# Taking eleven masks off the matrix engine, and moving two small jobs from VectorE to GpSimd

## The chip, the cores and the metric

The kernel runs on one core of one Trainium2 chip. The metric is the device time of one execution in microseconds (us), as a median of several runs. The engines are named as in the profile: PE is TensorE's matmul, PEld its weight load, DVE is VectorE, ACT is ScalarE, POOL is GpSimd, SP is SyncE, whose queue issues all transfers.

## What is computed

Attention with a window of 32 positions in eight batches of eight heads (half of the heads plain, half with a dilation of 4), followed by a gated two-layer network on the resulting tokens. Cut to what matters:

```python
# q, k, v: (8, 8, 576, 64) float32
scores = matmul(q, k.transpose(0, 1, 3, 2)) / sqrt(64)
mask_plain = (rel >= 0) & (rel < 32)                       # heads 0 to 3
mask_dil = (rel >= 0) & (rel < 128) & (rel % 4 == 0)       # heads 4 to 7
scores = where(mask, scores, -1e9)
scores = scores - max(scores, axis=-1)
attn = exp(scores); attn = attn / (sum(attn, axis=-1) + 1e-9)
x = (attn @ v), heads side by side                         # 4608 tokens x 512
h = x @ w_in                                               # 512 x 2048
g = h * clip(h + 3, 0, 6) / 6
out = g @ w_out                                            # 2048 x 512
```

The products of the network are made in float32 precision from pairs: a number is a high word in TensorE's shorter format and a low word, its remainder, and a product is three matmuls (high by high, high by low, low by high).

## The kernel before

**Tiles.** Attention is cut into 48 units that the program calls trios (a batch, plain or dilated, and a third of the sequence). Since the window is 32, a trio needs only small blocks of scores: 24 products of 32 rows by 64 columns, which lie side by side in one PSUM bank of 128 x 384. The network's tokens are cut into 12 chunks of 384. The first four chunks go through both layers in the plain way (`gemm1`, `gemm2`); the other eight are taken two by two, in four groups, with seven products in place of eight for each two-by-two step (`first_product`, `multiply_right`). For that the weights are needed in sums and differences as well: for each side (`w_in` is 0, `w_out` is 1) and each of eight pairs of weight blocks, `combine` adds high and low words of two blocks (`combo_words`, twice), makes four sums (`combo_sum`), splits them again and writes them to memory, from where PE's later stage loads them into a ring of eight places (`ring`).

**Stages.** A beginning with an order written out by hand handles the first 12 trios, the conversion of the weights and most of the first two chunks; it ends near 150 us. Behind it, until about 333 us, come the remaining plain products, and at eight places (`SPOTS`) a block of two trios (`attend`). Then come the four groups; in the first three, one more trio's block stands beside each first product of a pair of weight blocks, until all 36 later trios are done. A block of trios also holds the weights-by-values products of the trios two numbers earlier.

**A later trio, step by step.** PE makes the scores (`mm_scores`, L228). The mask, 0 or -1e30, gets on in one of two ways: for the trios numbered in `PE_MASKS` (counted from 0 behind the first twelve) PE first multiplies the mask table by an identity into the same bank (L338), and the scores are summed on top; for the others VectorE adds the mask and writes the result to SBUF (`add_mask`, L254), which frees the bank. Then `scaled_largest` takes six maxima per row (L280) and multiplies them by minus the scale (L281), ScalarE makes six exponentials with these as bias (L289), VectorE transposes blocks (L385, L386), ScalarE copies the crossing blocks (L393), and the result `a` is read by PE (L246). For a trio in `PE_MASKS` the bank stays taken until the last exponential. The values' product goes the same way: shares, transposes, crossing copies to `xf`, and GpSimd's copies into a token block `raw` or a subtraction of high words (L454, L456).

**What sets the order.** Behind the beginning, every operation of the later stages is put on a list with its engine, an assumed duration, what it must follow, and the places in pools that it takes and gives. PE's order is the order of the list. For DVE, ACT, POOL and SP a planner (`_in_time`) walks through time and takes for each engine the operation that can start first, and among those the most urgent. So a change of an engine or of an assumed duration reorders the queues of all engines but PE. Each engine works strictly in its order: an instruction that waits holds up all that is behind it.

**On GpSimd before.** In the later stages it makes the high words of the plain chunks' gates (L557) and the copies of tokens, and nothing else.

Of the kernel before, what the change touches and what calls it, by code (L numbers as in the profile page):

```python
# [37 lines left out]
EVER = 1.0e6  # L38
SLACK = 0.4
SPOTS = ((35, 1), (38, 1), (41, 1), (44, 1), (47, 1), (50, 1), (53, 1), (56, 1))  # L40
SPARE = ((0, 1, 1, 2, 1, 1, 2, 1), (1, 1, 2, 1, 0, 0, 1, 1))
LEAD_SUMS = 300.0
# [1 line left out]
LATER = 2  # L44
LANDING = 2.6
EARLY = 90.0
PE_MASKS = frozenset((2, 5, 8, 9, 11, 12, 13, 14, 15, 20, 29, 36, 37))
SHARED = frozenset((0, 1, 2, 3, 4, 7, 8, 9, 10, 11, 12, 13, 14, 15, 27, 28, 32))
WIPED = set()
POOL_LOWS = frozenset((10, 11))  # L50
# [36 lines left out]
def windowed_attention_ffn(ctx: ExitStack, tc: tile.TileContext, qk, vp, w, mask, out, out_t):  # L87
# [23 lines left out]
    nc = tc.nc  # L111
# [17 lines left out]
    SCALE = 1.0 / math.sqrt(D)  # L129
# [3 lines left out]
    wpool = ctx.enter_context(tc.tile_pool(name="wpool", bufs=SLOTS_W))  # L133
    work = ctx.enter_context(tc.tile_pool(name="work", bufs=WORK))
    loads = ctx.enter_context(tc.tile_pool(name="loads", bufs=NLOAD))
    small = ctx.enter_context(tc.tile_pool(name="small", bufs=2))
    ps_h = ctx.enter_context(tc.tile_pool(name="ps_h", bufs=2, space=bass.MemoryType.PSUM))
    ps_a = ctx.enter_context(tc.tile_pool(name="ps_a", bufs=6, space=bass.MemoryType.PSUM))

# [44 lines left out]
    def w_tile(name, shape, dtype=F32):  # L184
        return wpool.tile([P, *shape], dtype, name=name, tag="w")
# [22 lines left out]
    pss, pvs, tps = {}, {}, {}  # L208
# [11 lines left out]
    def by_tensor(t):  # L220
        return t < NFIRST or t - NFIRST in PE_MASKS

# [28 lines left out]
    def add_mask(t):  # L251
        _, kind, part = trios[t]
        es[t] = work_tile("e")
        return nc.vector.tensor_tensor(out=es[t], in0=pss[t][0][:, :CH], in1=mask_sb[:, 3 * kind + part], op=ALU.add)  # L254
# [16 lines left out]
            in1=mx.rearrange("p (s o) -> p s o", o=1).broadcast_to([P, SLOTS, 2 * QB]), op=ALU.subtract,  # L271
        )

    def scaled_largest(t):
        ps, masked = pss[t]
        if not masked:
            ps = es[t]
        mx = small.tile([P, SLOTS], F32, name="mx")
        pss[t] = ps, mx, masked
        nc.vector.tensor_reduce(out=mx, in_=ps[:, :CH].rearrange("p (s x) -> p s x", x=2 * QB), axis=AX.X, op=ALU.max)  # L280
        nc.vector.tensor_scalar_mul(mx, mx, -SCALE)  # L281

    def exponents(t, j):
        ps, mx, masked = pss[t]
        if not j and masked:
            es[t] = work_tile("e")
        for i in (2 * j, 2 * j + 1):
            cols = slice(2 * QB * i, 2 * QB * (i + 1))
            nc.scalar.activation(es[t][:, cols], ps[:, cols], AF.Exp, bias=mx[:, i : i + 1], scale=SCALE)  # L289
# [242 lines left out]
    phs, ts, ghs, gls, po, done = {}, {}, {}, {}, {}, set()  # L532
# [99 lines left out]
    def combo_words(side, k, i, eng):  # L632

        if (side, k) not in combos:
            combos[side, k] = w_tile("v", [4, HALF])
        x, v = (win, wout)[side][2 * k + i], combos[side, k]
        eng.tensor_tensor(
            out=v[:, 2 * i : 2 * i + 2].rearrange("p a n -> p (a n)"), in0=x[:, 0].bitcast(F32), in1=x[:, 1].bitcast(F32), op=ALU.add
        )
# [151 lines left out]
    def op(engine, us, do, after=(), lag=0.0, takes=(), gives=(), before=(), ahead=AHEAD):  # L791
        plan.append(Operation(engine, us, do, [x for x in after if x is not None], lag, [(*x, 0)[:3] for x in takes], list(gives), list(before), ahead))
        if engine == "PE":
            beats.append(len(plan) - 1)
        return len(plan) - 1

    def transfer(us, size, do, after=(), takes=(), gives=(), ahead=EVER):
        x = op("SP", us, do, after, takes=takes, ahead=ahead)
        return op("DMA", size * 1.3, lambda: None, [x], lag=LANDING, gives=gives, ahead=EVER)
# [18 lines left out]
    def attend(bs, pools):  # L818

        scores = [NFIRST + b for b in bs if NFIRST + b < T]  # L820
        values = [NFIRST + b - 2 for b in bs if b >= 2]
        couples = [(NFIRST + b, NFIRST + b - 2) for b in bs]
        order = [t for x in couples for t in x if t in scores + values]
        bank, room = dict(zip(order, pools)), {}

        def do():
            for x in couples:
                block(*(t if t in bank else None for t in x), [bank.get(t) for t in x])

        names = {x: "ps_h" if bank[x] is ps_h else "ps_a" for x in order}  # L830
        for x in names.values():
            room[x] = room.get(x, 0) + 1
        beat = op(
            "PE", 0.35 + 0.3 * sum(by_tensor(t) for t in scores) + 0.535 * len(order), do,
            [*(x for t in values for x in turned[t]), *(landed_k.get(t) for t in scores), *(landed_v.get(t) for t in values),
             *(freed.pop(0) for _ in range(room.get("ps_a", 0)) if freed), *released["ps_h"][-2:][: room.get("ps_h", 0)]],
            takes=list(room.items()), gives=[("work", len(values))],
        )
        for ts in scores:
            if by_tensor(ts):  # L840
                x = op("DVE", 0.68, lambda ts=ts: scaled_largest(ts), [beat], ahead=EVER)
            else:
                x = op("DVE", 0.55, lambda ts=ts: add_mask(ts), [beat], takes=ONE, gives=[(names[ts], 1)], ahead=EVER)
                released[names[ts]].append(x)
                x = op("DVE", 0.68, lambda ts=ts: scaled_largest(ts), [x], ahead=EVER)
            for i in range(3):
                holds = not i and by_tensor(ts)
                x = op(
                    "ACT", 0.54, lambda ts=ts, i=i: exponents(ts, i), [x], takes=ONE if holds else (),
                    gives=[(names[ts], 1)] if i == 2 and by_tensor(ts) else (), ahead=EVER,  # L850
                )
            if by_tensor(ts):
                released[names[ts]].append(x)
            turned[ts] = turn_over(ts, es, ats, "a", x)
            if ts + NLOAD < T:
                landed_k[ts + NLOAD] = transfer(0.4, 0.82, lambda ts=ts: load_qk(ts + NLOAD), [beat])
        for tv in values:
            if tv - NFIRST in SHARED:
                x = op("DVE", 0.35, lambda tv=tv: share(tv), [beat], ahead=EVER)
                for i in range(3):  # L860
                    x = op(
                        "ACT", 0.5, lambda tv=tv, i=i: shares(tv, i), [x], takes=() if i else ONE,
                        gives=[(names[tv], 1)] if i == 2 else (), ahead=EVER,
                    )
            else:
                x = op("DVE", 0.9, lambda tv=tv: normalise(tv), [beat], takes=ONE, gives=[(names[tv], 1)], ahead=EVER)
            released[names[tv]].append(x)
            x = turn_over(tv, xs, xfs, "xf", x)
            if tv + NLOAD < T:
                landed_v[tv + NLOAD] = transfer(0.4, 0.77, lambda tv=tv: load_v(tv + NLOAD), [beat])  # L870
            pieces = [(n, token // CH) for _, n, _, _, token in spans(tv)]
            x = [*x, ends_of[1]] if any(PLAIN <= c < PLAIN + 2 for n, c in pieces) else x
            touched = {c for n, c in pieces if c >= PLAIN + 2} - {c for c, kind in raw_seen if kind == trios[tv][1]}
            raw_seen.update((c, trios[tv][1]) for c in touched)
            plain = [n for n, c in pieces if c < PLAIN]
            if plain:
                x = [op("ACT", sum(0.15 + n / 500 for n in plain), lambda tv=tv: high(tv), x, ahead=EVER)]
            split[tv] = op(
                "POOL", sum(0.25 + n / 250 for n, _ in pieces), lambda tv=tv: low(tv, nc.gpsimd), x, takes=[("w", len(touched), 1)], gives=ONE, ahead=EVER
            )  # L880
# [23 lines left out]
    words, combined, taken = {}, {}, {}  # L904

    def combine(side, k):
        x = op("DVE", 0.69, lambda: combo_words(side, k, 0, nc.vector), takes=[("w", 2, SPARE[side][k])], ahead=LEAD_SUMS)
        words[side, k] = x = op("DVE", 0.69, lambda: combo_words(side, k, 1, nc.vector), [x], ahead=EVER)
        for i in range(4):
            x = op("DVE", 0.42, lambda i=i: combo_sum(side, k, i, nc.vector), [x], ahead=EVER)  # L910
        x = op("ACT", 1.05, lambda: combo_high(side, k), [x], ahead=EVER)
        x = op("DVE", 1.25, lambda: combo_low(side, k, 0, 1, nc.vector), [x], ahead=EVER)
        combined[side, k] = [
            transfer(0.9, 2.0, lambda: combo_out(side, k), [x], gives=[("w", 2)]),
            transfer(1.35, 1.5, lambda: combo_plain(side, k), ahead=EARLY),
        ]
# [362 lines left out]
    with tc.manual_schedule(  # L1279
# [3 lines left out]
        for name in ORDER.split():  # L1283
            name, _, behind = name.partition("@")
# [260 lines left out]
```

## Time and profile before

| what | value |
|---|---|
| median of 3 runs | 834.25 us (834.22 to 835.44) |
| the profiled execution | 834.65 us, its span 832.9 us |
| PE busy | 820.3 us, 98% of the span |
| VectorE busy | 646.8 us, 78% |
| ScalarE busy | 576.8 us, 69% |
| GpSimd busy | 117.0 us, 14% |
| moved by transfers | 214.71 MB, mean 258 GB/s |

A row of a group names line, engine, operation, the names of output and inputs, the shape and the count; behind the bar stand its busy time in us and the mean of one in ns, and then the idle time of the engine ahead of it with what ended it. A row of the waits names the instruction that waited, what it waited for, and then the total in us, the number of times and the longest. A row of the timeline has start and length in us, then engine, line and operation; its `x` counts neighbours that are shown as one. A row of stretches has for each engine the busy time and the number of instructions, then the granted clock, the share of the transfer engines and GB/s.

### The profile page before, as it was taken

The numbers are of one execution on the slowest core, as the hardware profiler recorded it, in microseconds if no ns is written. First come the engines' busy times: TensorE is split into PE (matmuls) and PEld (weight loads), VectorE is DVE, ScalarE is ACT, GpSimd is POOL, SyncE is SP. The second block draws the span as 40 slices with busy tenths as digits, with TensorE's granted clock in tenths as the row PEclk, the third lists the DMA queues.
The fourth block names the chain that finished last, engine by engine and source line by source line (L and its number), as shares of the span: only waits on it lengthen the run. The fifth ranks groups of instructions, "written<-read, shape, count | busy, mean of one in ns | idle before, by whom it ended". The sixth has DMA issues, their size and how long they took to land.

```text
span 832.9 us, 22207 instructions
## 1 busy us (share of the span) xinstructions
PE 820.3 (98%) x8743; PEld 773.0 (93%) x8743; DVE 646.8 (78%) x1291; ACT 576.8 (69%) x1406; POOL 117.0 (14%) x148
## 2 busy tenths in 40 slices
PE   7899999999999999999999999999999999999998
PEld 4688999898898888999999999999999999999998
DVE  4989996656788989888989786888776888445983
ACT  3788775244899884899965699955698845345552
POOL 1238442011222222001300000100001000000000
PEclk9999999999999999999999999999999999999999
DMA  8767433262679999999986799977788777896381
GB/s 279 250 201 243 126 109 120 76 223 98 205 227 305 300 344 382 342 395 392 384 295 235 257 334 306 348 253 260 256 313 306 252 267 256 305 358 229 124 297 57
DMA packets 115784, 214.71 MB, mean 258 GB/s; under 512 B 7520, under 2 KB 40288, under 8 KB 115680
## 3 DMA queue, kind: packets, MB, share of 16 engines
q1 hardware_dynamic: 115680, 213.29, 73.8%
q8 instruction: 69, 1.13, 0.5%
q14 instruction: 35, 0.29, 0.1%
HBM read 174.47 MB, written 38.80 MB: 256 GB/s over the span
## 4 chain that ended last, share of the span: by engine, by line
PE 93%; DVE 3%; DMA 2%; ACT 1%; issue 0%; SPq 0%; DVEq 0%
PE ps_o L742 28%; PE ps_x L751 10%; PE ps_x L753 9%; PE ps_x L752 9%; PE ps_o L593 5%; PE ps_o L594 5%; PE ps_o L592 5%; PE ps_h L542 5%; PE ps_h L544 5%; PE ps_h L543 5%; PE ps_b L246 2%; PE ps_b L228 1%; PE ps_a L246 1%; PE ps_a L228 1%; DMA st<-in_w 1%; DMA first<-in_v 1%
## 5 line engine op out<-in xcount | busy, mean ns | idle before, releaser
L742 PE MATMUL ps_o<-gh,ring 128*128 128x384 f32 x896 | 230.2, 334 | 0.0
L742 PEld LDWEIGHTS ps_o<-gh,ring 128*128 128x128 f32 x896 | 162.0, 188 | 0.0
L742 PE MATMUL ps_o<-gl,ring 128*128 128x384 f32 x448 | 149.7, 334 | 0.0
L1205 DVE TENSOR_TENSOR gl<-g,gh 128x384 fp32r<-128x384 f32 x224 | 115.7, 552 | 20.8 <-ACT gh L1201 19.8
L1201 ACT CAST gh<-g 128x384 fp32r<-128x384 f32 x224 | 104.7, 512 | 33.3 <-PE ps_o L742 25.1
L751 PE MATMUL ps_x<-x,ring 128*128 128x384 f32 x256 | 88.4, 345 | 0.0
L542 PE MATMUL ps_h<-x,wi 128*128 128x384 f32 x256 | 87.9, 343 | 0.0
L544 PE MATMUL ps_h<-x,wi 128*128 128x384 f32 x256 | 86.2, 337 | 0.2 <-DVE wi L526 0.2
L752 PE MATMUL ps_x<-x,ring 128*128 128x384 f32 x256 | 86.1, 336 | 0.0
L753 PE MATMUL ps_x<-x,ring 128*128 128x384 f32 x256 | 86.1, 336 | 0.0
L543 PE MATMUL ps_h<-x,wi 128*128 128x384 f32 x256 | 86.1, 336 | 0.0
L742 PEld LDWEIGHTS ps_o<-gl,ring 128*128 128x128 f32 x448 | 84.1, 188 | 0.0
L593 PE MATMUL ps_o<-wo,gh 128*128 128x512 f32 x192 | 74.8, 390 | 0.5 <-DVE wo L526 0.5
L592 PE MATMUL ps_o<-wo,gh 128*128 128x512 f32 x192 | 74.9, 390 | 0.0
L594 PE MATMUL ps_o<-wo,gl 128*128 128x512 f32 x192 | 74.7, 389 | 0.0
L456 POOL COPY raw<-xf 128x96 f32<-128x96 f32 (+2 forms) x65 | 29.4, 522 | 297.9 <-ACT xf L393 281.0
L550 ACT ACTIVATE t<-ps_h,three 128x384 f32<-128x384 f32 x64 | 37.0, 581 | 48.8 <-PE ps_h L544 48.6
L491 POOL TENSOR_SCALAR va<-st 128x512 f32<-128x512 f32 x32 | 55.6, 1748 | 76.0 <-DMA st<-in_w 55.0
L753 PE MATMUL ps_x<-cell,ring 128*128 128x384 f32 x192 | 64.9, 338 | 0.0
L751 PE MATMUL ps_x<-cell,ring 128*128 128x384 f32 x192 | 64.7, 337 | 0.0
L752 PE MATMUL ps_x<-cell,ring 128*128 128x384 f32 x192 | 64.7, 337 | 0.0
L1170 DVE TENSOR_TENSOR g<-g 128x768 f32<-128x768 f32 x64 | 60.9, 952 | 0.0
(113 smaller groups left out, 1801.1 us busy)
## 6 DMA issues: line engine op xcount, KB each, us to landing
ring<-sums SPq DMA_DIRECT2D x112, 512.0 KB, 8.4
ring<-rights SPq DMA_DIRECT2D x112, 512.0 KB, 7.0
st<-in_w SPq DMA_DIRECT2D x32, 512.0 KB, 4.4
kq<-in_qk SPq DMA_DIRECT2D x39, 416.0 KB, 5.2
v<-in_v SPq DMA_DIRECT2D x39, 390.0 KB, 5.9
sums<-wi SPq DMA_DIRECT2D x24, 256.0 KB, 6.5
rights<-wo SPq DMA_DIRECT2D x24, 256.0 KB, 5.4
out<-o SPq DMA_DIRECT2D x15, 384.0 KB, 2.8
```

The costliest lines, as they stand in the source:

```text
L542: nc.tensor.matmul(ph, lhsT=wt(f, 0)[:, ks], rhs=a, start=(kt == 0), stop=False)
L543: nc.tensor.matmul(ph, lhsT=wt(f, 0)[:, ks], rhs=b, start=False, stop=False)
L544: ins = nc.tensor.matmul(ph, lhsT=wt(f, 1)[:, ks], rhs=a, start=False, stop=(kt == NK - 1))
L592: nc.tensor.matmul(po[c][tt], lhsT=gh[:, rows], rhs=wt(f, 2), start=first, stop=False)
L593: nc.tensor.matmul(po[c][tt], lhsT=gh[:, rows], rhs=wt(f, 3), start=False, stop=False)
L594: return nc.tensor.matmul(po[c][tt], lhsT=gl[:, rows], rhs=wt(f, 2), start=False, stop=(f == NF - 1))
L742: nc.tensor.matmul(banks[part][:, :CH], lhsT=right[:, a, cols], rhs=x, start=(start and not i), stop=(i == 2), skip_group_check=True)
L751: nc.tensor.matmul(bank, lhsT=tile_[:, 0, ks], rhs=h[:, kt], start=(start and kt == 0), stop=False, skip_group_check=True)
L752: nc.tensor.matmul(bank, lhsT=tile_[:, 0, ks], rhs=l[:, kt], start=False, stop=False, skip_group_check=True)
L753: nc.tensor.matmul(bank, lhsT=tile_[:, 1, ks], rhs=h[:, kt], start=False, stop=(kt == 1), skip_group_check=True)
L1201: nc.scalar.copy(two[0], gated_tile(g, q, k))
L1205: nc.vector.tensor_tensor(out=two[1], in0=gated_tile(g, q, k), in1=two[0].bitcast(F32), op=ALU.subtract)
```

## The change

Three things. The table of later trios whose mask PE writes is emptied, so VectorE adds all of those masks. The product of the maxima by minus the scale moves from VectorE to GpSimd and becomes an operation of its own with an assumed 0.3 us; the maxima's own assumed duration falls from 0.68 to 0.55, and the pool of those small tiles goes from two places to four. The additions of high and low words in `combine` move from VectorE to GpSimd, with an assumed 1.4 us in place of 0.69. Sums, differences and the split that follow stay on VectorE and ScalarE.

```diff
-PE_MASKS = frozenset((2, 5, 8, 9, 11, 12, 13, 14, 15, 20, 29, 36, 37))
+PE_MASKS = frozenset()
...
-    small = ctx.enter_context(tc.tile_pool(name="small", bufs=2))
+    small = ctx.enter_context(tc.tile_pool(name="small", bufs=4))
...
-    def scaled_largest(t):
+    def plain_largest(t):
         ps, masked = pss[t]
         if not masked:
             ps = es[t]
         mx = small.tile([P, SLOTS], F32, name="mx")
         pss[t] = ps, mx, masked
         nc.vector.tensor_reduce(out=mx, in_=ps[:, :CH].rearrange("p (s x) -> p s x", x=2 * QB), axis=AX.X, op=ALU.max)
-        nc.vector.tensor_scalar_mul(mx, mx, -SCALE)
+
+    def scaled(t):
+        mx = pss[t][1]
+        nc.gpsimd.tensor_scalar_mul(mx, mx, -SCALE)
...
         for ts in scores:
-            if by_tensor(ts):
-                x = op("DVE", 0.68, lambda ts=ts: scaled_largest(ts), [beat], ahead=EVER)
-            else:
+            x = beat
+            if not by_tensor(ts):
                 x = op("DVE", 0.55, lambda ts=ts: add_mask(ts), [beat], takes=ONE, gives=[(names[ts], 1)], ahead=EVER)
                 released[names[ts]].append(x)
-                x = op("DVE", 0.68, lambda ts=ts: scaled_largest(ts), [x], ahead=EVER)
+            x = op("DVE", 0.55, lambda ts=ts: plain_largest(ts), [x], ahead=EVER)
+            x = op("POOL", 0.3, lambda ts=ts: scaled(ts), [x], ahead=EVER)
...
-        x = op("DVE", 0.69, lambda: combo_words(side, k, 0, nc.vector), takes=[("w", 2, SPARE[side][k])], ahead=LEAD_SUMS)
-        words[side, k] = x = op("DVE", 0.69, lambda: combo_words(side, k, 1, nc.vector), [x], ahead=EVER)
+        x = op("POOL", 1.4, lambda: combo_words(side, k, 0, nc.gpsimd), takes=[("w", 2, SPARE[side][k])], ahead=LEAD_SUMS)
+        words[side, k] = x = op("POOL", 1.4, lambda: combo_words(side, k, 1, nc.gpsimd), [x], ahead=EVER)
```

Up to the first block of a later trio PE's order is the same. Line numbers behind L274 grow by three with the change.

## The prediction

> **What bounds the kernel now.** First the page: the span and busy shares, then the chain that ended last.
>
> ```profile
> span 832.9 us, 22207 instructions
> PE 820.3 (98%) x8743; PEld 773.0 (93%) x8743; DVE 646.8 (78%) x1291; ACT 576.8 (69%) x1406; POOL 117.0 (14%) x148
> PE 93%; DVE 3%; DMA 2%; ACT 1%; issue 0%; SPq 0%; DVEq 0%
> ```
>
> TensorE carries 93% of the chain. A busy PE is not a proof that it never waits, so the second view is what PE waited for, and the third the chain in order of time (start, length, what).
>
> ```profile
> PE ps_a L355 <- DVE x L316: 3.6, 4, 1.5
> PE ps_h L544 <- DVE wi L526: 0.2, 1, 0.2
> 152.23 0.44 PE ps_h L544
> ```
>
> The waits on L355 belong to the hand-ordered beginning (its transposes of the first twelve trios). The last of the list, on L526, ends at 152.23 us, and the chain then stays on PE. So from there on a matmul that is taken out comes off the time, and work on VectorE, ScalarE or GpSimd costs only what makes PE wait. All of the change lies behind that point.
>
> **What is taken off PE.** Thirteen numbers stand in the old table, but there are only 36 later trios (numbered from 0), so 36 and 37 name none. The trace has eleven full-height mask matmuls, and at two places they read so:
>
> ```profile
> L338 PE MATMUL ps_a<-mi x17: 331/332/498, 4.9 to 299.0; 32*128 32x384 bf16 x12, 128*128 128x384 bf16 x5
> L338 PE MATMUL ps_b<-mi x6: 336/337/337, 207.3 to 503.0; 128*128 128x384 bf16 x6
> 221.99 0.39 PE L594 MATMUL ps_o<-wo,gl 128*128 128x512 f32 x1
> 224.79 0.44 PE L542 MATMUL ps_h<-x,wi 128*128 128x384 f32 x1
> 237.04 0.39 PE L594 MATMUL ps_o<-wo,gl 128*128 128x512 f32 x1
> 239.56 0.45 PE L542 MATMUL ps_h<-x,wi 128*128 128x384 f32 x1
> 251.83 0.39 PE L594 MATMUL ps_o<-wo,gl 128*128 128x512 f32 x1
> 252.06 0.34 PE L338 MATMUL ps_b<-mi 128*128 128x384 bf16 x1
> 254.81 0.44 PE L542 MATMUL ps_h<-x,wi 128*128 128x384 f32 x1
> 358.07 0.34 PE L753 MATMUL ps_x<-cell,ring 128*128 128x384 f32 x1
> 359.45 0.45 PE L751 MATMUL ps_x<-x,ring 128*128 128x384 f32 x1
> 366.69 0.34 PE L753 MATMUL ps_x<-cell,ring 128*128 128x384 f32 x1
> 368.24 0.44 PE L751 MATMUL ps_x<-x,ring 128*128 128x384 f32 x1
> ```
>
> The 0.34 us of a mask matmul is not its price, since PE overlaps matmuls. The price is the difference between blocks with and without it, from the last matmul ahead to the first behind. A block of two trios takes 2.52 us without masks (237.04 to 239.56), 2.80 with one in the middle (from 221.99) and 2.98 with both (from 251.83); a block of one takes 1.38 without and 1.55 with. So a mask in the middle is 0.28, both are 0.46, one in front is the rest, 0.18, and one in a single block 0.17. The two-trio blocks hold masks for trios 2, 5, 8 and 9, 11, 12 and 13, 14 and 15 (an even number stands in front): 0.18 + 0.28 + 0.46 + 0.28 + 0.46 + 0.46 = 2.12 us. Trios 20 and 29 stand in single blocks: 0.34. **Removed: 2.46, say 2.4 us.** An upper bound is the step from a mask to the next matmul start, about 0.27 each at most places (252.06 is one; the next start there is 252.33 in a row below): 11 x 0.27 = 3.0.
>
> How the program shows it, TensorE at the block of 251.83 us (`ps_o` is the output product, `mi` the mask table, `ps_a<-v,a` values and `ps_b<-kq` scores). Before:
>
> ```order
> L593 MATMUL ps_o_2489<-wo_2161,gh_3486 128x512
> L594 MATMUL ps_o_2489<-wo_2161,gl_3505 128x512
> L338 LDWEIGHTS mi_90
> L338 MATMUL ps_b_3571<-mi_90 128x384
> L246 MATMUL ps_a_3572<-v_3412,a_3511 32x65
> L228 MATMUL ps_b_3571<-kq_3404 32x64
> ```
>
> With the change:
>
> ```order
> L596 MATMUL ps_o_2489<-wo_2161,gh_3485 128x512
> L597 MATMUL ps_o_2489<-wo_2161,gl_3490 128x512
> L246 MATMUL ps_a_3566<-v_3415,a_3517 32x65
> L228 MATMUL ps_b_3565<-kq_3405 32x64
> L246 MATMUL ps_a_3566<-v_3415,a_3517 32x65
> ```
>
> Only the mask and its weights are gone; the product order stays.
>
> [...] These rows give groups (busy us, mean ns), or minimum/median/maximum ns, then one stretch (PE, PEld, DVE, ACT, POOL, granted clock, DMA).
>
> ```profile
> L254 DVE TENSOR_TENSOR e<-ps_b,mi 128x384 f32<-128x384 f32 x22 | 11.9, 541 | 0.9 <-PE ps_b L228 0.9
> L281 DVE TENSOR_SCALAR mx<-mx x36: 171/172/748, 196.0 to 623.9; 128x6 f32<-128x6 f32 x36
> L637 DVE TENSOR_TENSOR v<-wo 128x512 f32<-128x512 f32 x16 | 10.8, 701 | 0.0
> L454 POOL TENSOR_TENSOR x<-xf,x 128x384 fp32r<-128x384 f32 x4 | 4.3, 1076 | 11.1 <-ACT x L448 11.1
> L768 POOL CAST ident<-mi 128x128 f32<-128x128 bf16 x1 | 0.3, 289 | 4.6 <-DMA mi<-in_mask 4.6
> L557 POOL CAST gh<-t x36: 505/544/1437, 163.8 to 329.9; 128x384 fp32r<-128x384 f32 x36
> L526 DVE TENSOR_TENSOR wi<-va,wi x16: 677/684/1509, 24.6 to 151.5; 128x512 fp32r<-128x512 f32 x16
> 260.00:333.00 73.00, 73.00 (x954) 65.00 (x955) 65.27 (x135) 56.39 (x163) 16.46 (x27) 1.00 0.99 341
> ```
>
> VectorE gains eleven mask adds, 11 x 0.54 = 6.0 us, and loses 32 word adds (10.8 for the 16 of `wo`, and as many of `wi` in the same shape: 21.6) and 36 small products (at 0.17 or more, some 6): about 22 us less. GpSimd gets the word adds. The trace has none of 512 columns there; 384 took 1.08, so between 1.08 and 1.43 (in proportion), and I take 1.35, since some of a short one's time is fixed: 43 us. [...] The small product on GpSimd is bounded by nothing (it replaces 0.17 on VectorE) and by the 0.29 of the 128x128 cast, plus a wait for a running add of up to 1.35; I take 0.3. GpSimd was busy 16.5 of 73 us in the densest stretch, so it has room: 43 us spread over about 180.
>
> GpSimd and VectorE do hold each other up: the same cast takes 505 to 1437 ns, the same subtraction 677 to 1509, the product of six columns 171 to 748. The longest excess on VectorE is 0.83 us, the usual one 0.01 (684 against 677). Between 0 and 32 x 0.83 = 27 us go back to VectorE; with the higher figure its load in 260 to 333 us stays about where it is, 65 of 73. I take a quarter, 7 us. [...] On PE's path none of it costs anything as long as the two covers below hold.
>
> **Cover one: scores to weights.** Behind each block run mask, maxima, small product, six exponentials, a transpose and four crossing copies, until the weights `a` are read two trios later. The block of 251.83 us needs no mask for its own trios 6 and 7, yet its order changes on ScalarE (`t` is a gate's activation, `xf` a finished trio). Before:
>
> ```order
> L289 ACTIVATE e_3416<-e_3416,mx_3449 128x64 x2
> L308 ACTIVATE x_3481<-ps_a_3278,z_3454 128x64 x2
> L550 ACTIVATE t_3521<-ps_h_3463,three_92 128x384
> L393 COPY a_3511<-a_t_3512 32x192 x4
> L393 COPY a_3517<-a_t_3518 32x192 x4
> L393 COPY xf_3538<-xf_t_3539 32x192 x4
> ```
>
> With the change:
>
> ```order
> L292 ACTIVATE e_3407<-e_3407,mx_3421 128x64 x2
> L292 ACTIVATE e_3413<-e_3413,mx_3429 128x64 x2
> L553 ACTIVATE t_3515<-ps_h_3463,three_92 128x384
> L396 COPY xf_3509<-xf_t_3510 32x192 x4
> L396 COPY a_3517<-a_t_3518 32x192 x4
> L396 COPY a_3536<-a_t_3537 32x192 x4
> ```
>
> Four `xf` copies move ahead of both `a`. The trace of before there:
>
> ```profile
> 247.60 2.95 ACT L393 COPY a<-a_t 32x192 f32<-32x192 f32 x8
> 250.57 1.44 ACT L393 COPY xf<-xf_t 32x192 f32<-32x192 f32 x4
> 252.33 0.24 PE L246 MATMUL ps_a<-v,a 64*32 64x65 f32 x1
> 253.70 0.24 PE L246 MATMUL ps_a<-v,a 64*32 64x65 f32 x1
> ```
>
> The first four `a` copies end near 249.1 and are read at 252.33: 3.2 us to spare; the second four end at 250.55 and are read at 253.70: 3.1. The moved copies take 1.44, and this block, with no masks of its own any more, reads its first and second weights 0.2 and 0.5 us sooner: about 1.5 and 1.2 are left. A trio whose mask moves has 0.54 to 1.1 more ahead of its maxima (its own add and its partner's) and 0.3 more for the product. Together that stays inside 1.5 at most places. Below nothing it cannot go, since PE waits for no weights now; if the whole margin is eaten and one word add of 1.35 lies in front, a block waits some 1 us. I take **0.2 us** in all.
>
> **Cover two: ScalarE's queue.** If maxima come late, everything behind the exponentials waits, the seed copies of the later stage above all:
>
> ```profile
> 358.45 0.46 ACT L1079 COPY ps_x<-ps_x 128x384 f32<-128x384 f32 x1
> 361.64 0.34 PE L751 MATMUL ps_x<-x,ring 128*128 128x384 f32 x1
> 304.09 1.10 POOL L557 CAST gh<-t 128x384 fp32r<-128x384 f32 x1 [2.71 <-DVE t L553]
> 310.78 0.39 PE L592 MATMUL ps_o<-wo,gh 128*128 128x512 f32 x1
> ```
>
> The copy ends at 358.91 and its bank is overwritten by PE at 361.64: 2.7 us. The casts that now share GpSimd with the word adds end 5.6 us before they are read (305.19 to 310.78), and two word adds in a row are 2.7. So neither term costs PE anything by itself.
>
> GpSimd's queue at about 270 us shows who stands behind whom (`v` is the sum of words, `mx` the maxima, `raw` a copied token block):
>
> ```order
> L459 COPY raw_3995<-xf_3825 128x192
> L459 COPY raw_3426<-xf_3825 128x2x48
> L640 TENSOR_TENSOR v_4010<-wi_1836 128x512
> L284 TENSOR_SCALAR mx_4004<-mx_4004 128x6
> L284 TENSOR_SCALAR mx_4008<-mx_4008 128x6
> L560 CAST gh_4044<-t_4021 128x384
> ```
>
> A word add stands right ahead of two products of maxima: there the exponentials can wait about 1.35 us. Before, raw copies and casts alone stood in this queue.
>
> **The sum.** The profiled execution took 834.65 us, 1.75 around its span of 832.9, and is 0.4 above the median of the three runs, 834.25. Span 832.9 - 2.4 + 0.2 = 830.7; with 1.75 around it 832.4; as a median **832.1 us**, 0.26% less.
>
> **The rivals.** *The chain eats it.* The margins of cover one go at several blocks, where mask, partner's mask and word add add up (0.54 + 0.54 + 0.3 + 1.35 = 2.7 against 3.1, less what is moved ahead on ScalarE, 1.44): 1.2 us late each at most. Five of the eight early blocks at 0.4 are 2 us: 834.25 - 2.4 + 2.0 = 833.9. For it: ScalarE is busy 56 of 73 us and VectorE 65 there. Against: VectorE sheds 22 us less what the sharing takes.
>
> *GpSimd's queue stalls behind a transfer: slower.* A raw copy waits for a place that a transfer frees, and now maxima queue behind it.
>
> ```profile
> POOL raw L456 <- DMA ring<-rights: 10.6, 2, 6.0
> ```
>
> Two such waits existed, the longest 6.0 us, with nothing urgent behind. With maxima behind, ScalarE stands 6.0 and PE 6.0 - 2.7 = 3.3; two give 834.25 - 2.4 + 6.6 = 838.5. It decides from a wait of 2.7 us in front of maxima on. Against: both waits ended where GpSimd had nothing else to do, and may have been shorter at their own copy.
>
> *The sums come late.* The word adds take twice as long, and SyncE's queue sends weight sums ahead of the ring loads; each microsecond beyond the margin is PE's. Rows for the margin:
>
> ```profile
> ring<-sums SPq DMA_DIRECT2D x112, 512.0 KB, 8.4
> 317.42 4.69 SPq L686 DMA_DIRECT2D ring<-sums  x7
> 333.70 0.38 PE ps_x L751
> ```
>
> Seven loads issue from 317.42 on, so the first of them lands at about 325.8. The product that starts at 333.70 still reads the load before them, and the next one theirs, a microsecond later: some 9 us to spare. A pair of adds takes 1.3 us longer than before: hidden, unless SyncE stands more than 9 us; at 13, PE loses 4 and the time is 834.25 - 2.4 + 4 = 835.9.
>
> **How the numbers follow.** About 0.2% (1.7 us) is what a measurement can tell here. Forecast, under 0.7 us of new waits: 0.62. Chain eats it, within 0.2%: 0.22. Queue behind a transfer, slower: 0.10. Late sums, slower: 0.06. So faster 0.62, same 0.22, slower 0.16. The range: at the low end the upper bound of 3.0 and no wait, 831.3, and 0.4 for the spread of runs: 830.9. The high end takes in the second case and part of the slower ones: 835.2. The forecast's own range is 830.9 to 832.6.
>
> **What would show it.** Right: PE's waits after 152 us stay under 1 us, L338's successor has only the twelve first masks, blocks take 2.52 and 1.38 us. L640 on POOL at 1.1 to 1.5 us; L284 on POOL at 0.1 to 0.3, some at over 1; two-input VectorE instructions with longer maxima. The first wrong step would show as PE waiting at L246 on ScalarE's `a`; the third as exponentials idle behind POOL `mx`, and PE at L751 behind the seed; the last as PE waiting on `ring`. A word add over 2 us would overturn the covers.

## The result and the profile after

The changed kernel takes **845.71 us** (median of 4 runs, 845.11 to 847.95) against 834.36 for the kernel before on the same chip (4 runs, 834.22 to 835.44): a ratio of 1.014, 95% interval 1.0122 to 1.0158. It is 11 us slower where 2 us less were predicted, and the time lies outside the predicted range.

The page of the profile after; these lines answer to the first three that were shown of before:

```profile
span 843.5 us, 22171 instructions
PE 825.8 (98%) x8732; PEld 778.5 (92%) x8732; DVE 653.1 (77%) x1234; ACT 578.7 (69%) x1406; POOL 170.9 (20%) x216
PE 88%; DVE 5%; DMA 3%; ACT 1%; issue 1%; POOL 1%; SPq 0%; POOLq 0%; DVEq 0%
```

TensorE has eleven matmuls less (8732 for 8743), as said. But its share of the chain has gone from 93% to 88%. VectorE was to be rid of some 22 us and give 7 back; it is busy for 653.1 us, more than the 646.8 of before.

What TensorE waited for behind 150 us, of the kernel after. The kernel before had one wait of 0.2 us there:

```profile
PE ps_h L545 <- DVE t L556: 7.1, 2, 3.8
PE ps_a L246 <- ACT x L311: 0.7, 1, 0.7
```

Nearly all of the loss begins at two places, and neither is one that the prediction had named. L545 is a plain product's first matmul into a bank of `ps_h`, of which there are two. The bank is free once VectorE has made the gate `t` from it (L556). A block of two trios takes one of the two banks for the scores of its first trio (`attend` gets the pools `ps_h, ps_a, ps_a, ps_a`). So the first product behind a block needs the bank of the product just ahead of the block, and both waits are at such a product. The timeline of TensorE shows where (start, length; the idle time before it in brackets):

```profile
288.93 0.69 PE L545 MATMUL ps_h<-x,wi 128*128 128x384 f32 x1 [3.81 <-DVE t L556]
309.70 0.45 PE L545 MATMUL ps_h<-x,wi 128*128 128x384 f32 x1 [3.32 <-DVE t L556]
```

The same place in the kernel before. Its gate ended 2.3 us ahead of the matmul, and at the second place 2.8 us; at all eight blocks the margin was 1.35 to 3.12 us:

```profile
282.23 0.56 DVE L553 SCALAR_TENSOR_TENSOR t<-t,ps_h 128x384 f32<-128x384 f32 x1
283.93 1.38 DVE L645 TENSOR_TENSOR v<-v 128x256 f32<-128x256 f32 x3
285.09 0.44 PE L542 MATMUL ps_h<-x,wi 128*128 128x384 f32 x1
```

What stood ahead of that gate on VectorE, in the kernel after, ahead of the first of the two:

```profile
280.65 0.51 DVE L556 SCALAR_TENSOR_TENSOR t<-t,ps_h 128x384 f32<-128x384 f32 x1
281.08 1.05 DVE L648 TENSOR_TENSOR v<-v 128x256 f32<-128x256 f32 x2
282.06 1.62 DVE L564 TENSOR_TENSOR gl<-t,gh 128x384 fp32r<-128x384 f32 x1
283.61 3.36 DVE L648 TENSOR_TENSOR v<-v 128x256 f32<-128x256 f32 x3
288.36 0.52 DVE L556 SCALAR_TENSOR_TENSOR t<-t,ps_h 128x384 f32<-128x384 f32 x1
```

And GpSimd in the same stretch:

```profile
281.32 0.54 POOL L560 CAST gh<-t 128x384 fp32r<-128x384 f32 x1 [2.35 <-DVE t L556]
281.82 1.45 POOL L640 TENSOR_TENSOR v<-wi 128x512 f32<-128x512 f32 x1
283.23 1.58 POOL L640 TENSOR_TENSOR v<-wo 128x512 f32<-128x512 f32 x1
284.78 1.45 POOL L640 TENSOR_TENSOR v<-wi 128x512 f32<-128x512 f32 x1
```

Between two gates VectorE has a low half `gl` (L564) and five sums (L648), with four transposes behind them. The second gate's input from ScalarE was there at 284.39 us (`t`, L553, 0.60 from 283.79 on); it started at 288.36, behind all of these. In the kernel before a `gl` takes 0.56 us and a sum 0.42 (medians). Here the `gl` takes 1.62, from 282.06 to 283.68, as long as the word add beside it runs (281.82 to 283.27) and a little more; three sums take 3.36 where three took 1.38 before, and two adds run beside them. These two rows alone are 1.06 and 1.98 us longer. By groups (minimum/median/maximum ns), for the kernel after:

```profile
L648 DVE TENSOR_TENSOR v<-v x64: 385/424/1526, 164.0 to 350.2; 128x256 f32<-128x256 f32 x64
L564 DVE TENSOR_TENSOR gl<-t,gh x64: 511/559/1650, 44.7 to 342.9; 128x384 fp32r<-128x384 f32 x64
L556 DVE SCALAR_TENSOR_TENSOR t<-t,ps_h x64: 511/548/556, 42.6 to 341.1; 128x384 f32<-128x384 f32 x64
L640 POOL TENSOR_TENSOR v<-wi x16: 1269/1446/1737, 149.7 to 284.8; 128x512 f32<-128x512 f32 x16
L284 POOL TENSOR_SCALAR mx<-mx x36: 229/236/802, 196.8 to 635.0; 128x6 f32<-128x6 f32 x36
```

The two groups that read twice from SBUF have maxima some three times as long as their medians. All nine sums over 1 us have a word add beside them on GpSimd. The gate itself, which takes one input from PSUM, never took more than 0.56.

The waits of 7.1 us are not all. TensorE's clock, in stretches of the kernel after that are cut where the granted clock changes (length, then busy time of PE, PEld, DVE, ACT, POOL, then granted clock, share of the transfer engines, GB/s):

```profile
283.75:287.16 3.41, 1.26 (x96) 0.99 (x94) 3.38 (x4) 1.69 (x3) 2.47 (x2) 1.00 0.70 207
287.16:290.58 3.42, 1.65 (x5) 1.66 (x6) 3.42 (x8) 2.74 (x8) 1.64 (x2) 0.50 0.87 216
290.58:293.99 3.41, 3.41 (x11) 3.21 (x11) 2.56 (x5) 0.88 (x4) 3.38 (x9) 0.50 1.03 367
307.64:311.06 3.42, 1.36 (x8) 1.36 (x9) 3.42 (x9) 1.70 (x5) 1.35 (x2) 1.00 0.95 318
311.06:314.47 3.41, 3.41 (x11) 3.04 (x10) 3.41 (x5) 3.35 (x7) 2.45 (x4) 0.50 1.00 310
```

At 0.50 the matmuls of L545 to L547 start every 0.32 us (290.05, 290.37, 290.69), where at 1.00 they start every 0.17 (278.40, 278.57, 278.74 in the kernel before). Behind the first wait TensorE works at this half speed for 1.65 + 3.41 = 5.1 us, behind the second, after some 1.4 us at full speed, for 3.4. By these rows that costs 5.06 x 0.50 = 2.5 us and 3.41 x 0.50 = 1.7 us. The account is then 7.1 + 4.2 + 0.7 = 12.0 us, of which the masks that are gone give some back.

To see in which part of the program a kernel loses, the span behind the beginning is cut at four matmuls of TensorE: part 1 runs from the first score of the first later block to the first block of one trio, part 2 to the last such block of the first group, part 3 to the first block of the next group, part 4 to the end. Lengths in us, from the profiled execution of each kernel:

| kernel | part 1 | part 2 | part 3 | part 4 |
|---|---|---|---|---|
| before | 139.2 | 60.5 | 67.9 | 372.0 |
| after | 149.7 | 60.4 | 68.0 | 371.6 |

The loss is all in part 1. Ahead of part 1 TensorE makes the same matmuls in every kernel here, and they still took 191.1 to 195.4 us from one execution to the next. So single times of unchanged work differ by some microseconds in the comparisons below, and the lengths of the four parts tell more than a time does.

### The profile page after: what moved, and what is told of

The parts are those of the page before. It is cut to its first block, busy times and chain, and to the rows that moved or that the text cites. A ratio compares the mean times of both kernels' runs of the same rounds, so it can differ in the third digit from the quotient of the medians.

```text
span 843.5 us, 22171 instructions
## 1 busy us (share of the span) xinstructions
PE 825.8 (98%) x8732; PEld 778.5 (92%) x8732; DVE 653.1 (77%) x1234; ACT 578.7 (69%) x1406; POOL 170.9 (20%) x216
## 3 DMA queue, kind: packets, MB, share of 16 engines
q8 instruction: 69, 1.13, 0.5%
## 4 chain that ended last, share of the span: by engine, by line
PE 88%; DVE 5%; DMA 3%; ACT 1%; issue 1%; POOL 1%; SPq 0%; POOLq 0%; DVEq 0%
PE ps_o L745 28%; PE ps_x L754 10%; PE ps_x L756 9%; PE ps_x L755 9%; PE ps_o L596 4%; PE ps_o L597 4%; PE ps_o L595 4%; PE ps_h L545 4%; PE ps_h L547 4%; PE ps_h L546 4%; PE ps_b L246 2%; DVE v L648 2%; DMA st<-in_w 1%; PE ps_b L228 1%; PE ps_a L228 1%
## 5 line engine op out<-in xcount | busy, mean ns | idle before, releaser
L745 PE MATMUL ps_o<-gh,ring 128*128 128x384 f32 x896 | 230.5, 334 | 0.0
L745 PEld LDWEIGHTS ps_o<-gh,ring 128*128 128x128 f32 x896 | 162.1, 188 | 0.0
L745 PE MATMUL ps_o<-gl,ring 128*128 128x384 f32 x448 | 149.7, 334 | 0.0
L1204 ACT CAST gh<-g 128x384 fp32r<-128x384 f32 x224 | 105.1, 513 | 31.6 <-PE ps_o L745 22.6
L545 PE MATMUL ps_h<-x,wi 128*128 128x384 f32 x256 | 88.8, 347 | 7.1 <-DVE t L556 7.1
L547 PE MATMUL ps_h<-x,wi 128*128 128x384 f32 x256 | 87.2, 341 | 0.0
L546 PE MATMUL ps_h<-x,wi 128*128 128x384 f32 x256 | 87.2, 340 | 0.0
L745 PEld LDWEIGHTS ps_o<-gl,ring 128*128 128x128 f32 x448 | 84.1, 188 | 0.0
L553 ACT ACTIVATE t<-ps_h,three 128x384 f32<-128x384 f32 x64 | 36.9, 581 | 43.0 <-PE ps_h L547 42.6
L292 ACT ACTIVATE e<-e,mx 128x64 f32<-128x64 f32 x216 | 60.2, 347 | 3.5 <-POOL mx L284 3.3
L564 DVE TENSOR_TENSOR gl<-t,gh 128x384 fp32r<-128x384 f32 x64 | 51.6, 806 | 12.5 <-POOL gh L560 9.8
```

What stands on the lines that cost most here:

```text
L545: nc.tensor.matmul(ph, lhsT=wt(f, 0)[:, ks], rhs=a, start=(kt == 0), stop=False)
L546: nc.tensor.matmul(ph, lhsT=wt(f, 0)[:, ks], rhs=b, start=False, stop=False)
L547: ins = nc.tensor.matmul(ph, lhsT=wt(f, 1)[:, ks], rhs=a, start=False, stop=(kt == NK - 1))
L745: nc.tensor.matmul(banks[part][:, :CH], lhsT=right[:, a, cols], rhs=x, start=(start and not i), stop=(i == 2), skip_group_check=True)
L1204: nc.scalar.copy(two[0], gated_tile(g, q, k))
```

## Experiments

The theory, called A in the expectations: the word adds, reading on GpSimd, hold up VectorE's sums and low halves one for one; the gate behind them comes late, and with it the bank that it frees. The rivals have their letters in the expectations, which also put the two waits at 4.0 and 3.5 us, or 7.5 together; the trace has 3.81 and 3.32. Each kernel is compared with the kernel before on its own chip (medians 833.99, 834.10 and 834.88 us, 17 to 23 runs).

**The adds moved alone** (kernel before with nothing but this):

```diff
-        x = op("DVE", 0.69, lambda: combo_words(side, k, 0, nc.vector), ...
+        x = op("POOL", 1.4, lambda: combo_words(side, k, 0, nc.gpsimd), ...
```

> The kernel before with its word adds moved to GpSimd, and nothing else; eleven masks stay on PE. A: VectorE's sums of 256 columns reach 1.4 us or more as in the change, PE waits some 4 to 10 us in the stretch from 270 to 315 us, the time is 840 to 848. C: no more than 835.

Measured: 843.64 us, ratio 1.0103 (1.0087 to 1.012). What TensorE waited for in this kernel:

```profile
PE ps_h L542 <- DVE t L553: 3.8, 3, 1.8
PE ps_h L542 <- ACT e L289: 2.9, 1, 2.9
```

And its sums, by group:

```profile
L645 DVE TENSOR_TENSOR v<-v x64: 374/419/1514, 162.0 to 347.1; 128x256 f32<-128x256 f32 x64
```

This one part of the change brings most of the loss (9.7 of some 11 us), with the same stretched sums and waits for the same two banks; part 1 is 150.0, and the others are as before. The first three waits are for the gate. The fourth, of 2.9 us, is for the other bank, which a trio that TensorE masks holds until its last exponential (`e`). Its maxima stand on VectorE behind a sum of 1.50 us beside an add, so here too VectorE is what was held up.

**All but the adds** (the change with the adds back on VectorE, the edit above in reverse):

> The change with its word adds put back on VectorE; all masks by VectorE and the product of the maxima on GpSimd stay. Theory A (GpSimd's word adds and VectorE's two-input instructions hold each other up, so the gates that free PE's banks come late): PE's two waits of 4.0 and 3.5 us go, the time is 834.4 - 2.4 + 0 to 0.5 = 832.0 to 832.5. Rival C (the longer way from scores to weights, masks on VectorE and the product on GpSimd, makes PE wait): the waits stay, 840 or more.

Measured: 835.5 us, ratio 1.0012 (0.9994 to 1.0029). The waits at the gate are gone, as the theory has it, and part 1 is 137.1, 2.1 shorter than before. But the time misses the theory's 832.0 to 832.5, and part 3 is 71.1 where it was 67.9, with waits of TensorE that neither theory had:

```profile
PE ps_o L745 <- ACT gh L1204: 1.3, 2, 0.8
```

So the gain from the masks is there, and is given back at about 400 us, in the second products of the first group.

**The same order without reading.** Each word add becomes three fills of its output with a constant; the sums of words are left out, so the weight sums and what follows from them are not the reference's. Lengths that the planner assumes, and with them every queue's order, are those of the change.

```diff
-        eng.tensor_tensor(out=v[:, 2 * i : 2 * i + 2]..., in0=x[:, 0]..., in1=x[:, 1]..., op=ALU.add)
+        for _ in range(3):
+            eng.memset(v[:, 2 * i : 2 * i + 2]..., 0.5)
```

> The change in the same order, with each word add on GpSimd replaced by three memsets of the same place, which write and read nothing; the sums of high and low words are left out, so the sums of weights are constants. A (the two engines meet where both read): VectorE's sums of 256 columns stay under 0.5 us, PE's waits on the gate vanish, 832.0 to 833.5. Rival B (the new order of the queues makes PE wait, whatever GpSimd's instructions read): the waits stay, 843 to 847.

Measured: 833.22 us, ratio 0.998 (0.9968 to 0.9993). TensorE waits for nothing behind 160 us. The engines on its page:

```profile
PE 816.7 (98%) x8732; PEld 771.6 (93%) x8732; DVE 627.3 (75%) x1234; ACT 576.8 (69%) x1406; POOL 168.7 (20%) x280
```

Its fills and its sums, by group:

```profile
L641 POOL MEMSET v<- x96: 520/526/579, 151.9 to 309.0; 128x512 f32 x96
L647 DVE TENSOR_TENSOR v<-v x64: 382/419/805, 164.9 to 338.6; 128x256 f32<-128x256 f32 x64
```

Three fills take 1.58 us of GpSimd, more than an add, in the same places of the same queues, and VectorE's sums are as short as before. So neither GpSimd's load nor the new order of the queues makes the loss. What is left is that the adds read and that each is longer than one fill; the copies below, of nearly a fill's length, tell these two apart. The new order does use up margin: at the two places the gates end 0.36 and 1.34 us ahead of their matmuls here, where it was 2.3 and 2.8. VectorE is busy 627.3 us here and 653.1 in the change, the same 1234 instructions: **adds in place of fills cost it 25.8 us**. The groups that grew, of the kernel after (busy us, mean ns):

```profile
L564 DVE TENSOR_TENSOR gl<-t,gh 128x384 fp32r<-128x384 f32 x64 | 51.6, 806 | 12.5 <-POOL gh L560 9.8 <-ACT gh L560 2.6
L648 DVE TENSOR_TENSOR v<-v 128x256 f32<-128x256 f32 x64 | 36.6, 602 | 1.7 <-POOL v L640 1.2
```

The same groups of the kernel with fills:

```profile
L564 DVE TENSOR_TENSOR gl<-t,gh 128x384 fp32r<-128x384 f32 x64 | 39.8, 623 | 14.9 <-POOL gh L560 12.2 <-ACT gh L560 2.6
L647 DVE TENSOR_TENSOR v<-v 128x256 f32<-128x256 f32 x64 | 27.0, 450 | 4.6 <-DMA sums<-wi 2.7 <-POOL v L641 1.2
```

The low halves take 11.8 of it and the sums 9.6. The few long ones that are left have a GpSimd instruction beside them that reads: the longest sum, 0.81 us, a subtraction of high words and a cast. The four lengths are 137.3, 60.5, 67.9 and 371.8: 637.5 together where the kernel before has 639.6. That puts the worth of the masks at 2.1 us, from one execution of each; the medians differ by 0.8 and the ratio's interval reaches from 0.6 to 2.7 us. Part 1 is 12.4 us shorter than in the change; the account above has 12.0 of it.

**The same order, reading one input at a time.** Each add becomes two copies of one word each; the sum is left out here as well.

```diff
-        eng.tensor_tensor(out=v[:, 2 * i : 2 * i + 2]..., in0=x[:, 0]..., in1=x[:, 1]..., op=ALU.add)
+        for word in range(2):
+            eng.tensor_copy(out=v[:, 2 * i : 2 * i + 2]..., in_=x[:, word]...)
```

> The change in the same order, with each word add on GpSimd replaced by two copies of one word each to the same place, which read one input and not two; the sum is left out. If it is reading by GpSimd as such that holds up VectorE's two-input instructions, the sums of 256 columns still reach 1 us or more and PE still waits on the gate: 838 to 847, by how long two copies are (0.51 us for 384 columns gives 0.7 each, 1.4 together). If only GpSimd's two-input instructions do it, 832 to 834.

Measured: 836.39 us, ratio 1.003 (1.0014 to 1.0045). What TensorE waited for behind 150 us:

```profile
PE ps_h L545 <- DVE t L556: 3.7, 2, 2.5
```

Its copies, by group:

```profile
L641 POOL COPY v<-wi x32: 607/615/1492, 148.3 to 282.2; 128x512 f32<-128x512 f32 x32
```

The result lies between what the two theories expected. The waits are half of the change's, for the same gate, and part 1 is 141.0, 3.7 more than with fills; the clock stayed at 1.00. Reading one input at a time holds VectorE up too. The longest sum, 0.83 us, hardly tells it, since 0.81 occurs with fills; the mean does (546 against 450 ns), and 18 sums are over 0.7 us, 17 of them beside a copy, where the kernel with fills has two. VectorE is busy for 638.3 us, 11 more than with fills. A copy takes 0.61 us at the least and a fill 0.53, so it is the reading and not the length that does it; that a copy holds it up for less than an add fits its length (an add takes 1.27 at the least).

**Adds cut in two.** The order is again the change's, and each add is two of 256 columns, so each hold should be half as long:

```diff
+        for h in range(2):
+            cols = slice(h * HALF, (h + 1) * HALF)
+            eng.tensor_tensor(out=v[:, 2 * i + h], in0=x[:, 0, cols]..., in1=x[:, 1, cols]..., op=ALU.add)
```

> The change with each word add on GpSimd cut in two of 256 columns, in the same place of the queue; nothing else. A, with an instruction holding up the other engine for its own length: a half takes some 0.8 us, a sum on VectorE of 0.42 waits for at most that, so its longest falls from 1.53 to about 1.2; VectorE gets through twice as many sums per pair of adds, PE's waits of 7.5 us fall under 3, 836 to 840. If only GpSimd's total time counts: 843 to 848.

Measured: 840.61 us, ratio 1.0063 (1.004 to 1.0087); part 1 is 146.1. Its sums, by group:

```profile
L648 DVE TENSOR_TENSOR v<-v x64: 385/422/974, 163.6 to 346.0; 128x256 f32<-128x256 f32 x64
```

What TensorE waited for behind 150 us:

```profile
PE ps_h L545 <- DVE t L556: 5.6, 2, 3.1
```

Half right. The longest sum falls from 1.53 to 0.97 us, as a hold of half the length says. But the waits are 5.6 us in all, more than the expected 3, and the time is just above the expected range. There are twice as many holds, and GpSimd's adds sum to more (two halves of at least 0.72 make 1.44, against 1.27); that this is the reason is not shown.

**Only the early adds on GpSimd.** The seven pairs whose adds come first stay on GpSimd; the nine that fall into the crowded stretch go back:

```diff
+EARLY_SUMS = frozenset(((0, 0), (0, 1), (0, 2), (0, 3), (0, 4), (1, 4), (1, 5)))
+        engine, us, eng = ("POOL", 1.4, nc.gpsimd) if (side, k) in EARLY_SUMS else ("DVE", 0.69, nc.vector)
```

> The change with the word adds of nine of the sixteen pairs, those that fell between 270 and 320 us, back on VectorE; seven pairs, mostly ahead of 270 us, stay on GpSimd. A: the waits at 285 and 306 us vanish, VectorE's sums of 256 columns over 1 us are few; 832 to 833.5 if the waits near 400 us of the run with all adds on VectorE stay away too, 834 to 836 if they come (VectorE then has the load of these nine pairs). B (the order of the change as such): 840 or more.

Measured: 844.41 us, ratio 1.0128 (1.0113 to 1.0143): a miss in the time. What TensorE waited for:

```profile
PE ps_o L746 <- ACT gh L1206: 3.4, 2, 2.7
PE ps_h L546 <- DVE t L557: 1.8, 1, 1.8
```

The waits at the gate fall from 7.1 to 1.8 us, and part 1 from 149.7 to 141.0, which is the theory's side of it. What is won there is lost in part 3 (75.3 for 68.0), at the place of the second experiment and with the clock down as well (0.50 from 405.92 to 412.75 us).

**The masks alone** (kernel before with an empty `PE_MASKS`):

> The kernel before with all later masks on VectorE, and nothing else. A: PE loses eleven mask matmuls, 834.4 - 2.4 = 832.0, plus up to 1 us since VectorE has 6 us more to do and no relief: 832.0 to 833.0. C: PE waits for weights or gates between 200 and 310 us, 835 or more.

Measured: 838.33 us, ratio 1.0046 (1.0032 to 1.0059). Part 1 is 137.4, 1.8 less than before, and part 3 72.8, 4.9 more. Both theories missed this: the time is one that C allowed, but TensorE does not wait between 200 and 310 us. The longest of TensorE's waits:

```profile
PE ps_o L742 <- ACT gh L1201: 2.6, 3, 1.2
```

The chain of work from 396 to 410 us, by line, and ScalarE's crossing copies `xf` of finished trios in part 3, in the kernel before and in this one:

```profile
by line: ACT xf L393 50.1%; ACT t L1006 12.7%; ACT gh L1201 11.4%; issue 10.5%; ACT s L1048 5.6%; DVE gl L1205 4.9%; DVE xf L386 3.4%; PE ps_o L742 3.1%; ACTq L1006 0.1%
L393 ACT COPY xf<-xf_t 32x192 f32<-32x192 f32 x21 | 7.4, 350 | 0.4
L393 ACT COPY xf<-xf_t 32x192 f32<-32x192 f32 x40 | 14.0, 350 | 1.6 <-DVE xf L386 1.0
```

ScalarE has these copies among the high halves `gh` for which TensorE waits, and they are half of the chain there. All the kernels agree: with 13 to 21 such copies in part 3 it takes 67.9 to 68.0 us, with 30 to 40 of them 70.6 to 75.3.

**Five masks back** (the kernel "all but the adds", with trios 11 to 15 masked by TensorE again), to see whether VectorE's load from these masks is what makes part 3 longer:

```diff
-PE_MASKS = frozenset()
+PE_MASKS = frozenset((11, 12, 13, 14, 15))
```

> The product of the maxima on GpSimd, all word adds on VectorE, masks of trios 11 to 15 left on PE, those of the other six (2, 5, 8, 9, 20, 29) on VectorE. Theory D (the waits near 400 us of the runs with all masks and adds on VectorE come from what its queue is behind by then): VectorE has 3 us less to do than there, the waits shrink, PE keeps 0.18 + 0.28 + 0.46 + 0.34 = 1.26 us of saved matmuls; 832.7 to 834.0 against 834.1 of the kernel before. If the waits come from the new order whatever VectorE's load, 834 to 836.

Measured: 835.48 us, ratio 1.0009 (0.9998 to 1.002), part 3 is 70.7, and the wait `PE ps_o L745 <- ACT gh L1204` is 1.3 us in two pieces, as with no mask at all. VectorE's load from those five is not the cause. Part 3 holds 30 of the copies `xf` here. That the planner has put them off into part 3 is seen; which earlier event makes it do so stays open.

**The small product alone** (kernel before with the product of the maxima on GpSimd and four places for it):

> The kernel before with the product of the maxima on GpSimd and four places for it, and nothing else; eleven masks stay on PE, the word adds on VectorE. A: no new wait, 833.5 to 835.0, no change beside the kernel before. C (the product on GpSimd makes the way to the weights too long): PE waits at the blocks, 836 or more.

Measured: 835.3 us, ratio 1.001 (0.9997 to 1.0022). TensorE has no wait behind 150 us, and the four parts are 139.2, 60.6, 67.9 and 372.0: no cost and no gain that can be told.

**The planner told of longer sums:**

```diff
-            x = op("DVE", 0.42, lambda i=i: combo_sum(side, k, i, nc.vector), [x], ahead=EVER)
+            x = op("DVE", 1.45, lambda i=i: combo_sum(side, k, i, nc.vector), [x], ahead=EVER)
-        x = op("DVE", 1.25, lambda: combo_low(side, k, 0, 1, nc.vector), [x], ahead=EVER)
+        x = op("DVE", 2.0, lambda: combo_low(side, k, 0, 1, nc.vector), [x], ahead=EVER)
```

> The change with other assumed durations for the planner alone: 1.45 in place of 0.42 us for a sum of 256 columns and 2.0 in place of 1.25 for the split's low half on VectorE, as the change's trace has them beside a word add; no instruction is another. A with the gates' place in VectorE's queue as the way to PE: fewer sums stand ahead of a gate, PE's waits of 7.5 us shrink to under 3, 834 to 839. If the holding up alone sets it, whatever the order: 843 to 847.

Measured: 857.94 us, ratio 1.0288 (1.0273 to 1.0304): a larger loss, and a miss of both expectations. What TensorE waited for:

```profile
PE ps_b L246 <- ACT a L396: 17.4, 2, 17.2
```

VectorE's timeline ahead of that wait's end:

```profile
387.33 2.35 DVE L657 TENSOR_TENSOR v<-v,sh 128x1024 fp32r<-128x1024 f32 x2
395.25 2.36 DVE L657 TENSOR_TENSOR v<-v,sh 128x1024 fp32r<-128x1024 f32 x2 [0.82 <-ACT sh L652]
398.11 0.56 DVE L254 TENSOR_TENSOR e<-ps_b,mi 128x384 f32<-128x384 f32 x1
```

The gate's waits do shrink to 0.9 us, and part 1 is 138.5. But the work that the planner now takes for long is put off: splits stand bunched at 387 to 397 us ahead of a block's mask (L254), and TensorE waits 17.2 us for weights. Longer assumed durations did not make a better order.

## Why the prediction was wrong

**The step that failed** is the sentence "On PE's path none of it costs anything as long as the two covers below hold", by which the sum put what GpSimd costs VectorE at nothing. Both covers held: TensorE waited neither for the weights `a` nor behind ScalarE's seed copies. Yet it waited 7.1 us for VectorE's gate and lost 4.2 more to the clock behind these waits.

**Under it stood a term of the wrong size**, "I take a quarter, 7 us" for what VectorE gives back. It measured 25.8 us, close to the upper bound of 27 that stood beside it. Beside the quarter stood a usual excess of 0.01 us. The median behind it (684 ns, with 677 as the shortest) is of rows from 24.6 to 151.5 us, from the beginning; and in the stretch where most of the adds were to go, GpSimd was busy for only 16 of 73 us. Such a median tells how often the two met before the change, not what a meeting costs; the maxima (1437, 1509) told that. With the word adds the two meet much more often: 18 of the 32 adds start between 271 and 319 us, mostly one behind the other, and a low half `gl` whose cast `gh` is GpSimd's starts just as GpSimd goes on to its next instruction, often an add (12 of the 13 low halves over 1 us behind 140 us have an add beside them). So the median was the wrong measure, and a VectorE held up for as long as the word adds run should have been a rival with a chance. Only its estimate for all 32 adds at their full length, 32 x 1.35 = 43 us, would have been too high.

**A cover was missing.** The prediction watched the weights `a` and ScalarE's queue. It did not ask which banks TensorE waits for VectorE to free in that stretch, the two of `ps_h` behind the gate, where 1.35 to 3.12 us of margin stood in the trace of before. Some 22 us less in sum were no help: the time comes back in the densest stretch, where VectorE was busy 65 of 73 us before. That stretch in the kernel after (PE, PEld, DVE, ACT, POOL, granted clock, transfers):

```profile
260.00:333.00 73.00, 65.05 (x847) 58.44 (x847) 68.47 (x114) 53.47 (x158) 44.04 (x49) 0.93 0.96 327
```

VectorE is busy for 68.5 of 73, TensorE for 65 at a mean clock of 0.93. In the kernel that only fills, VectorE is busy for 62.6.

**The sizes that held.** The masks are worth about what the blocks said: 2.1 us by the parts for 2.4. Blocks without masks take 2.49 and 1.37 us in the kernel after (2.52 and 1.38 were read). A word add takes 1.45 (1.35), the small product 0.24 (0.3), and moved alone it costs nothing that can be told. At L246 there was one wait of 0.7 us where 0.2 was set down for new waits; it was not for the weights `a` but for a bank of `ps_a` from which ScalarE still read (`x`, L311).

**The rivals.** None of the three came: no matmul waited for the weights, the small products ran within 0.2 us of their maxima where the profile names a transfer, and no matmul waited for `ring`. The rival on the slow side that was needed (VectorE's sums held up until a gate is late, at the price of two waits and the clock behind them) was not among them. Two of the named signs did show: two-input VectorE instructions with longer maxima, and TensorE's waits above 1 us.

**Cover one, in part.** The forecast had no term for a new order of the queues in the first group. The masks alone cost 0.46%, with ScalarE's copies `xf` put off into part 3. So without the adds, too, the gain of 2.1 us in part 1 was not kept (835.5 against 834.0). In the change itself part 3 is 68.0, so this is no part of its loss.

## What to carry to other kernels

Before work with two inputs goes to GpSimd, count which two-input VectorE instructions will run beside it, and take the longest of the rows, not the median, for each meeting (here 32 x 0.83 = 27 us, where 25.8 came); a move that empties VectorE in sum can fill it where it matters (here 68.5 of 73 us, where it was 65.3). List every buffer that the waiting engine gets back from the engine that is slowed down, PSUM banks among them. Where a planner writes the queues, a local edit has to be priced at all later stages, since a changed order can take back the gain in a later one (the masks alone: part 1 1.8 us shorter, part 3 4.9 us longer).

## What the runs showed of the hardware

- In the kernel after, 21 sums and low halves, which read twice from SBUF, started beside a word add more than 0.1 us ahead of its end. All 21 lasted until the add had ended and a little longer: the nine sums 0.28 to 0.29 us, the twelve low halves 0.41 to 0.42. A sum of 0.42 us took up to 1.53 beside adds of 1.45 and up to 0.97 beside halves; beside copies the mean of the sums was 0.55. With fills, which only write, it was 0.45, and 0.46 in the kernel before (longest sum 0.81 and 0.80).
- A wait of TensorE can cost more than itself: behind the waits of 7.1 us at the gate it worked 8.5 us at a clock of 0.50, which by the rows above cost 4.2 more. Behind 150 us, the granted clock of the kernel after changes only at 287.16, 293.99, 311.06 and 314.47, whole multiples of 3.41 us apart. Where TensorE, at the full clock, stood for 2.15 and 2.05 us of the 3.41 ahead of such a change (rows of 283.75 and 307.64 above), and for 1.75 in the first row below, the clock was 0.50 in the stretch behind. It came back to 1.00 behind stretches in which TensorE was busy for all 3.41 us (those that end at 293.99 and 314.47). No threshold is shown: in the beginning of the kernel before, the clock was 0.50 from 30.62 us on behind a stretch of 3.42 in which TensorE stood for 1.31. The first two rows are of the kernel with the adds moved alone (one gap of 1.75). The other two are of the one with copies: its gap of 2.47 falls into both rows with 1.34 and 1.13, and the clock stayed at 1.00. That these rows are cut where its clock could have changed is the author's estimate, counted on in steps of 3.41 us from the clock's change at 37.25 us of that trace:

```profile
282.26:285.67 3.41, 1.66 (x99) 1.34 (x99) 3.38 (x9) 1.75 (x4) 0.75 (x2) 1.00 0.68 166
285.67:289.09 3.42, 3.42 (x12) 3.42 (x11) 3.39 (x6) 3.14 (x7) 2.84 (x8) 0.50 0.97 308
296.66:300.08 3.42, 2.08 (x166) 1.87 (x158) 3.42 (x6) 1.34 (x2) 2.91 (x5) 1.00 1.10 376
300.08:303.49 3.41, 2.28 (x13) 2.28 (x14) 3.41 (x7) 2.64 (x8) 2.20 (x3) 1.00 1.00 341
```
